# Forming one operand (T4) of a Strassen-type matmul by DMA: a copy and an accumulating transfer on the GpSimd queue, in place of one VectorE subtraction

## The chip, the cores and the metric

One core of one Trainium2 chip. The metric is the device time of one execution in microseconds (us). TensorE (PE) multiplies, VectorE (DVE) works elementwise, ScalarE (ACT) empties PSUM, GpSimd (POOL) does little but issue transfers here, and SyncE (SP) issues most transfers. Sixteen DMA engines serve all queues.

## The reference

```python
# x0: 16384 x 1024, ws: 6 x 1024 x 1024, bs: 6 x 1024, all bf16
x = x0
for l in range(6):
    proj = einsum('bd,de->be', x, ws[l]) + bs[l]
    x = x0 * proj + x
```

## The kernel before

The rows are cut into 16 pairs of blocks of 512 rows ("row pairs"). A *unit* is one layer of one row pair: 96 units. In a unit the product of x and the layer's weights is done by a Strassen-Winograd scheme with seven half-size products (P1 to P7) in place of eight; in 89 *steady* units P2 and P5 are split once more the same way. The units of the first row pair and the very last unit use one level only.

The scheme needs sums of blocks of x, formed on DVE, and sums of weight blocks. The weight sums are formed on DVE during the first row pair, stored to HBM (`Lc`), and loaded from there by all later pairs. Order on the engines is fixed by a table of ranks.

```python
B11, B12, B21, B22 = blk(xs, 0, 0), blk(xs, 0, 1), blk(xs, 1, 0), blk(xs, 1, 1)
ttop("T1", T[1][:], B12, B11, SUB, [XI[0, 1], XI[0, 0]], ["T1"])
ttop("T2", T[2][:], B22, T[1][:], SUB, [XI[1, 1], "T1"], ["T2"])
ttop("T3", T[3][:], B22, B12, SUB, [XI[1, 1], XI[0, 1]], ["T3"])
ttop("T4", T[4][:], B21, T[2][:], SUB, [XI[1, 0], "T2"], ["T4"])
# ... (cut)
for m in range(KH):
    group(f"P6.{m}", "6", pA[m], A[m], T[2], ["T2", A[m]], m, False)
    # ... P3, P7 and the emptying of PSUM (cut)
    group(f"P4.{m}", "4", pA[m], A[m], T[4], ["T4", A[m]], m, False)   # last group of a unit
```

Each tile T is 128 partitions x 2048 bf16 = 512 KB. x0 of the next row pair is loaded by transposing DMAs, and the finished x of the last row pair goes out by transposing DMAs and stores. All of these stand on SyncE's queue with the weight loads (nine of 512 KB per unit, into a ring of 16 tiles). They fall into the first three units of each row pair.

```python
if l == (2 if pr == 0 else 0) and nxt < NPAIR:
    for n in range(2):
        # ... x0 of the next pair, transposed on its way in
        op(base + 23 + n, ld, [], XN)
```

## Time and profile before

The time was 2276.61 us (2 runs, 2276.53 to 2276.68).

| one steady unit, 23.4 us | busy us |
|---|---|
| PE | 23.4 |
| DVE | 21.5 |
| ACT | 19.2 |
| POOL | 0 |

The page of the kernel before, in parts: busy time by engine; two DMA queues (packets, MB, share of the time of 16 engines; q1 is SyncE's, q0 GpSimd's); and the chain of work that ended last.

```profile
PE 2265.4 (100%) x12951; PEld 1264.0 (56%) x12951; DVE 2079.9 (91%) x2326; ACT 1839.4 (81%) x3228; POOL 22.1 (1%) x43
...
q1 hardware_dynamic: 618864, 534.58, 79.1%
q0 software_dynamic: 5184, 18.88, 2.2%
...
PE 98%; DVE 1%; SPq 0%; DMA 0%; issue 0%; ACT 0%; DVEq 0%
```

PE is busy all the time and is the chain. DVE is busy for 91% but is not on the chain. A DMA share is the sum of the packets' times; packets overlap, so it can pass 100%.

Groups by shape of the kernel before, DVE only (count, then busy us and mean ns). The first and the third line are T2 and T4 together, from x or, in layer 1, from x0.

```profile
L198 DVE TENSOR_TENSOR T<-xst,T 128x2048 bf16<-128x2048 bf16 x160 | 194.5, 1216 | 0.0
...
L198 DVE TENSOR_TENSOR T<-x0T 128x2048 bf16<-128x2048 bf16 x32 | 39.0, 1218 | 3.7 <-DMA x0T<-in_x_dram 3.7
L198 DVE TENSOR_TENSOR T<-x0T,T 128x2048 bf16<-128x2048 bf16 x32 | 38.9, 1216 | 0.1
```

The DMA engines' load is uneven. In the first units of a row pair the share is around or above 1; in layers 4 to 6 it is 0.62. The same view shows the second row pair, the first steady one:

```profile
160.00:180.00 20.00, 20.00 (x108) 10.33 (x107) 19.44 (x22) 16.72 (x30) 0.53 (x1) 1.00 1.08 369
180.00:200.00 20.00, 20.00 (x122) 11.78 (x121) 18.18 (x21) 17.46 (x31) 0.00 (x0) 1.00 1.17 255
200.00:220.00 20.00, 20.00 (x122) 11.65 (x121) 18.20 (x22) 16.66 (x30) 0.00 (x0) 1.00 1.12 271
220.00:240.00 20.00, 20.00 (x122) 11.74 (x121) 18.33 (x22) 17.16 (x31) 0.00 (x0) 1.00 1.05 389
240.00:260.00 20.00, 20.00 (x120) 11.55 (x119) 18.23 (x22) 15.97 (x29) 0.00 (x0) 1.00 0.75 255
```

Here the share is 1.05 or more for 80 us on end. The last weight sums have just been stored, and the ring of weight tiles fills from HBM at once.

### The profile page before, as it was taken

To read this page: it belongs to the slowest core of one execution; us is meant where nothing else is said; L and a number is where in the kernel's file an instruction comes from. 1 tells how busy PE (TensorE), PEld (TensorE's weight loads), DVE (VectorE), ACT (ScalarE), POOL (GpSimd) and SP (SyncE) were. 2 spreads that over 40 slices of the span, in tenths; PEclk is the share of its full clock that TensorE was granted. 3 is DMA by queue.
4 is the path that set the end of the run, shared out by engine and by line. 5 is a ranking of instruction groups with operands and counts; after the bars stand their busy time and mean duration, and the time that the engine had idled before them with its cause. 6 is when DMAs were issued, how large, how long until landed. Compare 5 with 4: busy or idle time off the path is not lost.

```text
span 2275.2 us, 34978 instructions
## 1 busy us (share of the span) xinstructions
PE 2265.4 (100%) x12951; PEld 1264.0 (56%) x12951; DVE 2079.9 (91%) x2326; ACT 1839.4 (81%) x3228; POOL 22.1 (1%) x43
## 2 busy tenths in 40 slices
PE   9999999999999999999999999999999999999998
PEld 4455555555555555555555555555555555555554
DVE  7999999999999999999999999999999999999997
ACT  5678888888888888888888888888888888888887
POOL 1110000000000000000000000000000000000000
PEclk9999999999999999999999999999999999999999
DMA  9779797796977969779697796978969689696872
GB/s 279 229 270 289 261 242 269 219 301 209 252 257 221 288 217 260 250 226 283 213 274 241 228 283 204 273 245 230 283 200 292 226 232 286 194 303 216 241 240 65
DMA packets 625868, 557.01 MB, mean 245 GB/s; under 512 B 397600, under 2 KB 552224, under 8 KB 625696
## 3 DMA queue, kind: packets, MB, share of 16 engines
q1 hardware_dynamic: 618864, 534.58, 79.1%
q0 software_dynamic: 5184, 18.88, 2.2%
q8 instruction: 101, 1.65, 0.3%
q10 hardware_dynamic: 1648, 1.32, 0.2%
q14 instruction: 71, 0.58, 0.1%
HBM read 436.22 MB, written 52.43 MB: 215 GB/s over the span
## 4 chain that ended last, share of the span: by engine, by line
PE 98%; DVE 1%; SPq 0%; DMA 0%; issue 0%; ACT 0%; DVEq 0%
PE pA L285 57%; PE pX L389 24%; PE pX L285 16%; DVE ev L198 1%; SPq L529 0%; DMA wp<-in_ws_dram 0%; DVE xst L198 0%; DVE T L198 0%; DVE ti L198 0%; DVE wp L198 0%; SPq L538 0%; ACT ev L294 0%; DVE x0T L487 0%; DVEq L608 0%; DVEq L198 0%
## 5 line engine op out<-in xcount | busy, mean ns | idle before, releaser
L285 PEld LDWEIGHTS <-wp 128*128 128x128 bf16 x7904 | 772.3, 98 | 843.7 <-issue 3.9
L285 PE MATMUL pA<-T,wp 128*128 128x512 bf16 x4608 | 1054.9, 379 | 0.5 <-DVE T L198 0.5
L294 ACT ACTIVATE ev<-pA,b_all 128x512 bf16<-128x512 f32 x1124 | 704.8, 690 | 211.8 <-PE pA L285 211.4
L389 PEld LDWEIGHTS <-wp 128*128 128x128 bf16 x4984 | 487.1, 98 | 156.6 <-issue 15.2
L198 DVE TENSOR_TENSOR ev<-ev,x0T 128x2048 bf16<-128x2048 bf16 (+2 forms) x484 | 482.7, 999 | 8.1 <-ACT ev L294 1.5
L198 DVE TENSOR_TENSOR xst<-ev,xst 128x2048 bf16<-128x2048 bf16 x319 | 388.9, 1219 | 18.6 <-DVE ev L198 0.5
L389 PE MATMUL pX<-ti,wp 128*128 128x256 bf16 x2848 | 397.6, 272 | 0.0
L198 DVE TENSOR_TENSOR ev<-ev,ev 128x2048 bf16<-128x2048 bf16 (+1 forms) x283 | 343.7, 1215 | 26.7 <-ACT ev L294 9.8
L294 ACT ACTIVATE ev<-pX,b_all 128x512 bf16<-128x512 f32 x412 | 289.4, 705 | 59.9 <-PE pX L285 49.3
L285 PE MATMUL pX<-xst,wp 128*128 128x512 bf16 x1376 | 336.4, 379 | 0.0
L285 PE MATMUL pA<-xst,wp 128*128 128x512 bf16 x1280 | 313.5, 379 | 0.0
L290 ACT COPY pX<-pA 128x512 f32<-128x512 f32 x412 | 256.3, 625 | 44.7 <-PE pA L285 44.3
L290 ACT CAST ev<-pX 128x512 bf16<-128x512 f32 x384 | 224.8, 619 | 49.0 <-ACT ev L294 37.6
L198 DVE TENSOR_TENSOR ev<-iu,ip 128x1024 bf16<-128x1024 bf16 x178 | 122.4, 688 | 120.7 <-ACT iu L290 120.7
L290 ACT COPY pX<-pX 128x512 f32<-128x512 f32 x356 | 208.7, 587 | 8.4
L290 ACT CAST iu<-pX 128x512 bf16<-128x512 f32 x356 | 196.8, 639 | 0.0
L198 DVE TENSOR_TENSOR T<-xst 128x2048 bf16<-128x2048 bf16 x160 | 194.8, 1217 | 0.3
L198 DVE TENSOR_TENSOR T<-xst,T 128x2048 bf16<-128x2048 bf16 x160 | 194.5, 1216 | 0.0
L389 PE MATMUL pX<-T,wp 128*128 128x256 bf16 x1068 | 160.2, 273 | 0.0
L290 ACT CAST ip<-pX 128x512 bf16<-128x512 f32 x178 | 104.7, 589 | 54.1 <-PE pX L389 54.1
L389 PE MATMUL pX<-xst,wp 128*128 128x256 bf16 x888 | 133.2, 273 | 0.0
L198 DVE TENSOR_TENSOR xst<-ev,x0T 128x2048 bf16<-128x2048 bf16 x64 | 78.2, 1222 | 1.6
(44 smaller groups left out, 624.3 us busy)
## 6 DMA issues: line engine op xcount, KB each, us to landing
wp<-Lc SPq DMA_DIRECT2D x538, 512.0 KB, 4.6
wp<-in_ws_dram SPq DMA_DIRECT2D x285, 512.0 KB, 5.3
out_dram<-x0T SPq DMA_DIRECT2D x30, 1024.0 KB, 8.6
Lc<-wp POOLq DMA_DIRECT2D x24, 512.0 KB, 6.2
Lc<-isum POOLq DMA_DIRECT2D x12, 512.0 KB, 6.9
w<-in_ws_dram SPq DMA_DIRECT2D x5, 512.0 KB, 6.3
wp<-in_ws_dram ACTq DMA_DIRECT2D x2, 512.0 KB, 5.8
out_dram<-x0T SPq DMA_DIRECT2D x2, 512.0 KB, 3.6
```

What stands on the lines that cost most here:

```text
L198: nc.vector.tensor_tensor(out=o, in0=a, in1=b, op=op)
L285: nc.tensor.matmul(bank[:], lhsT=wt[(u, w)][:, k, m * P:(m + 1) * P], rhs=rhs[:, k, :], start=(start and k == 0), stop=(k == KH - 1), skip ...
L290: add(name, lambda: nc.scalar.copy(out=dst, in_=src), rd, wr)
L294: add(name, lambda: nc.scalar.activation(out=dst, in_=src, func=IDENT, bias=b_all[:, c:c + 1], scale=1.0), rd, wr)
L389: nc.tensor.matmul(pX[bank][:, m * NQ:(m + 1) * NQ], lhsT=wv[:, k, m * P:(m + 1) * P], rhs=rhs[:, k, :], start=(start and m == 0 and k == ...
```

## The change

Intent: DVE is 91% busy, so take one of its operations out of each steady unit. T4 = x21 - T2 becomes x21 + (-T2). T2 is formed negated, and the weight sum that it is multiplied with is negated to match, which adds no operation. x21 is copied to T4 by a plain DMA as soon as it exists, and the negated T2 is added by an accumulating DMA.

```diff
-            combo("6", "5", "1", SUB, ("5",))
+            combo("6", "1", "5", SUB, ("5",))
...
-            combo("3", "2", "6", SUB, ("6",))
+            combo("3", "2", "6", ADD, ("6",))
...
-        ttop("T2", T[2][:], B22, T[1][:], SUB, [XI[1, 1], "T1"], ["T2"])
+        ttop("T2", T[2][:], T[1][:], B22, SUB, [XI[1, 1], "T1"], ["T2"])
...
-        ttop("T4", T[4][:], B21, T[2][:], SUB, [XI[1, 0], "T2"], ["T4"])
+        if one:      # one-level units
+            ttop("T4", T[4][:], B21, T[2][:], ADD, [XI[1, 0], "T2"], ["T4"])
+        else:
+            add("d4", lambda B21=B21: nc.gpsimd.dma_start(T[4][:], B21), [XI[1, 0]], ["T4"])
+            add("T4", lambda: nc.gpsimd.dma_start(out=T[4][:], in_=T[2][:], accum_op=ADD), ["T2", "T4"], ["T4"])
```

(The rank table gains an entry for the copy, `d4@3.3`. Lines below the change move down by four, so L389 is L393 after, L504 is L508.)

More of the change, by code (lines that the diff above doesn't have):

```diff
@@ L33 @@
 E4.2@23.01 E4.3@23.59
-T1@-1.14 5t13@0.59 5t2@3.06 2t13@3.39 5t4@5.13 2t2@6.6 T2@6.93 2t4@8.07 T4@8.4 5cc@10.88 T3@11.48 2cc@12.61 Q1@13.35
+d4@3.3 T1@-1.14 5t13@0.59 5t2@3.06 2t13@3.39 5t4@5.13 2t2@6.6 T2@6.93 2t4@8.07 T4@8.4 5cc@10.88 T3@11.48 2cc@12.61 Q1@13.35
 Qm@14.62 Qa@15.89 Ua@17.43 Um@18.7 Ux@19.97 Va@21.11 Wma@23.38 Wmb@24.58 Wx@25.31 Vm@27.38 Vx@28.85
@@ L115 @@
 E4.3@23.28 E4.2@23.85
-T1@-8.81 5t13@-7.54 2t13@-6.94 2t2@-5.20 T2@-4.87 5t2@-3.40 5t4@.36 T4@2.97 2t4@5.58 T3@6.85 2cc@12.32 Q1@13.06
+d4@3.3 T1@-8.81 5t13@-7.54 2t13@-6.94 2t2@-5.20 T2@-4.87 5t2@-3.40 5t4@.36 T4@2.97 2t4@5.58 T3@6.85 2cc@12.32 Q1@13.06
 Qm@14.33 5cc@15.47 Qa@16.07 Ua@17.41 Um@18.68 Ux@19.95 Va@21.08 Wma@23.45 Wmb@24.66 Wx@25.40 Vm@27.47 Vx@28.94
@@ L126 @@
 E4.1@22.74 E4.2@23.61
-T1@-1.18 5t13@.65 5t2@3.13 2t13@3.47 5t4@5.20 2t2@6.67 T2@7.01 2t4@8.14 T3@8.48 T4@9.61 2cc@12.46 Q1@13.20 Qm@14.47
+d4@3.3 T1@-1.18 5t13@.65 5t2@3.13 2t13@3.47 5t4@5.20 2t2@6.67 T2@7.01 2t4@8.14 T3@8.48 T4@9.61 2cc@12.46 Q1@13.20 Qm@14.47
 5cc@15.61 Qa@16.21 Ua@17.45 Um@18.72 Ux@19.99 Va@21.12 Wma@23.49 Wmb@24.69 Wx@25.43 Vm@27.50 Vx@28.97
```

## The prediction

> **What bounds the kernel.** TensorE. The page has PE busy 2265.4 of 2275.2 us (100%) at a granted clock of 0.999; the chain of waits is 98% PE, 1% DVE. A steady unit takes 23.44 us (the timeline repeats at that distance); a window of 23.40 us has 23.40 us of PE, 21.55 of DVE, 19.25 of ACT, none of POOL. DVE's one idle spell in a unit is 1.37 us, waiting for ACT.
>
> **What the change removes.** 89 DVE operations (one per steady unit), 1.216 us each by the groups by shape: 108 us, so DVE falls from 91% to about 87%. First-pair units and the last unit keep their DVE T4. The built programs show PE order unchanged, and DVE order unchanged but for the 89 missing rows. None of this is on the chain, so removing it saves nothing. The swapped operands cost nothing.
>
> **What it adds.** 178 transfers of 512 KB on the GpSimd queue. POOL spends 0.53 us on each (36 such stores in the trace, issued while DVE was busy): 94 us on an idle engine. On the DMA engines one plain 512 KB store took 2.2% x 2275 / 36 = 1.4 us of all 16. The accumulating one must read two operands (the Trainium skill, "Collectives: The Full Stack", The bandwidth ceiling: the add needs two source reads); I estimate 2.8 us from the plain one. No accumulating transfer is in the trace before, so this is the weakest number. Together 89 x 4.2 = 374 us, DMA share from 82% to about 98%. That share is no ceiling: windows reach 1.25, and rates reach 399 GB/s against a mean of 245, so the weight traffic still fits. Weights are loaded some 30 us before use (issue times of SyncE against the units), and SyncE waits over 1,300 us for buffers to come free, so a delay of a few us is absorbed.
>
> **The deadline of T4.** From a unit's start: x21 is ready by +3.2, so the copy is issued at about +3.3 and lands, at the 6.2 us of the queue's stores, at about +9.5. T2 ends at +8.2. The accumulating transfer then runs from +9.5 to about +16.5. The first P4 matmul starts at +20.0: slack 3.5 us; before it was 10.3. In light stretches (DMA share 0.6) it should be larger; in three of six units (transposes, output stores; share 1.0 to 1.25, median landings of 8 to 9 us) it may vanish, and PE then waits 1 to 3 us in some units. I expect 0 to 30 us in all.
>
> **Prediction: 2279 us, 8 times in 10 within 2271 to 2315. Faster by over 2%: 0.01; within 2%: 0.85; slower by over 2%: 0.14.**
>
> **What would show it.** PE still about 100% busy, DVE down by 108 us, its idle time up by as much, in a gap after T2; POOL about 94 us more; the GpSimd queue's share up by some 16 points. Deadline step: the landing times of the two new transfers, and little or no idle time of PE that ends with a DMA into T. Weight step: no PE idle released by weight loads.
>
> **What would make it wrong.** (a) The accumulating transfer is much slower than two reads suggest (say 10 us of all engines): then every P4 waits, or the DMA engines run out, and the time rises by 5% or more. (b) Descriptor generation on GpSimd is held up by DVE's two-input operations; the 0.53 us speaks against it. (c) The heavy stretches delay T4 in half the units. A gain above 0.5% would mean DVE did hold PE up somewhere, which the waits do not show.

## More of the kernel before

Windows of one unit each, for four units of one row pair: layers 2, 3, 4, 5. Columns are length; PE, weight loads, DVE, ACT and POOL busy (with the number of instructions); granted clock, the share of its full clock that PE was given; DMA share; GB/s.

```profile
459.90:483.30 23.40, 23.40 (x138) 13.27 (x137) 21.51 (x25) 19.24 (x35) 0.00 (x0) 1.00 1.14 273
483.30:506.70 23.40, 23.40 (x137) 13.30 (x136) 21.51 (x26) 19.24 (x35) 0.00 (x0) 1.00 1.00 359
506.70:530.20 23.50, 23.50 (x138) 13.34 (x137) 21.61 (x26) 19.35 (x35) 0.00 (x0) 1.00 0.62 202
530.20:553.60 23.40, 23.40 (x137) 13.29 (x136) 21.52 (x26) 19.25 (x35) 0.00 (x0) 1.00 0.63 203
```

## The result, and the profile after

The changed kernel took 2302.98 us (2 runs, 2299.06 and 2306.9), a ratio of 1.0115 [1.0086, 1.0145]. A ratio is the mean time of one kernel's fast runs over that of the other's in the same rounds, so it is not quite the ratio of the quoted medians. Five more rounds (below) gave 2301.15 us against 2277.15. So the change costs 24 to 26 us, 1.0 to 1.2%.

The page after, in the same parts:

```profile
PE 2271.5 (99%) x12951; PEld 1263.7 (55%) x12951; DVE 1980.4 (86%) x2237; ACT 1839.7 (80%) x3228; POOL 149.1 (6%) x221
...
q1 hardware_dynamic: 618864, 534.58, 76.4%
q0 software_dynamic: 30816, 112.21, 17.9%
```

DVE is down by 99.5 us (89 operations of 1.216 us are 108 us, but consecutive ones overlap: they start 1.14 us apart), POOL is up, and q0 has 17.9% where it had 2.2%. That is (0.179 x 2305 - 0.022 x 2275) / 89 = 4.07 us of all 16 engines per T4; the prediction estimated 4.2.

DVE's idle time in a unit, by the timeline, before and then after (start, length, engine, line, operation; in brackets the idle time ahead of it and what ended it):

```profile
846.00 0.69 DVE L198 TENSOR_TENSOR ev<-iu,ip 128x1024 bf16<-128x1024 bf16 x1 [1.37 <-ACT iu L290]
```

```profile
866.11 0.69 DVE L198 TENSOR_TENSOR ev<-iu,ip 128x1024 bf16<-128x1024 bf16 x1 [2.52 <-ACT iu L290]
```

The time that was freed is 1.15 us more of waiting for ACT, at the place where T4 was formed. PE is the loser. The waits of PE and of its weight loads (PEld) in the change's trace: who, for whom, total us, times, longest us.

```profile
PEld L285 <- DMA wp<-Lc: 15.5, 2, 13.7
...
PE pA L285 <- DMA wp<-Lc: 13.2, 1, 13.2
...
PE pA L285 <- DMA T<-T: 8.0, 8, 2.1
...
PE pA L285 <- ACT ev L294: 1.0, 2, 0.8
```

None of these waits for DMA stands in the trace before. The two lines for `wp<-Lc` tell of one event at 221 to 234 us, seen by the weight load and by the matmul behind it (the weight load's line also counts a wait of 1.8 us at 175 us). In PE's timeline of the change:

```profile
219.05 1.90 PE L285 MATMUL pX<-xst,wp 128*128 128x512 bf16 x8
234.16 8.96 PE L285 MATMUL pA<-T,wp 128*128 128x512 bf16 x32 [13.21 <-DMA wp<-Lc]
```

PE stood still for 13.2 us, for one tile of weights. The 32 matmuls after it took 8.96 us where 32 of the same take 7.07 (line 197.26 of this timeline), because the clock had been halved. The Trainium skill ("TensorE: Matmul & The Clock Gate", The HAM clock gate) says that an idle PE falls to half clock and needs about 3.4 us of work to come back. The trace agrees: the two windows of 10 us from 220 to 240 us show a granted clock of 0.72 and 0.60.

SyncE's queue tells why that tile was late. Its timeline before, then after:

```profile
200.48 11.04 SPq L504 DMA_TRANSPOSE x0T<-in_x_dram  x2
211.62 0.53 SPq L246 DMA_DIRECT2D wp<-Lc  x1
```

```profile
207.57 15.96 SPq L508 DMA_TRANSPOSE x0T<-in_x_dram  x2
223.63 0.53 SPq L246 DMA_DIRECT2D wp<-Lc  x1
```

The load that PE waited for (issued at 223.63 and landed at 234) stands behind two transposing loads of x0. They were begun 7 us later and took 5 us longer to issue than before. So the load was issued 12 us later than it had been, and it landed (completed) after 10.5 us where it had taken 3.8. There was little room for that. In the trace before, this tile landed at 215.4 and its matmuls began at 218.46: a lead of 3.0 us, where the same tile of the third unit of the fourth row pair had 15.7.

The other waits are T4s that came late. The issue view of the change gives the median time from issue to landing:

```profile
T<-T POOLq DMA_DIRECT2D x89, 512.0 KB, 8.8
T<-xst POOLq DMA_DIRECT2D x74, 512.0 KB, 5.5
```

I laid the two traces side by side, unit by unit, by the start of each P1. Of the 29.8 us between these two profiled executions 15.3 us arise in the third unit of the second row pair, 1.5 us in its first unit, 0.8 us at the start of the kernel, and about 12 us in a dozen units scattered over the rest, 0.2 to 4 us each. Counted from a unit's start ("+" in what follows), the accumulating transfer landed at a median of +17.8 us (layers 4 to 6) and +18.2 us (layers 1 to 3); P4 begins at +20.0. Fifteen of 89 landed after +19.9. The nine of these in layers 4 to 6 were all in layer 4.

One of them shows the price of a short wait:

```profile
1531.59 3.62 PE L285 MATMUL pA<-T,wp 128*128 128x512 bf16 x16
1537.31 5.30 PE L285 MATMUL pA<-T,wp 128*128 128x512 bf16 x16 [2.10 <-DMA T<-T]
```

The wait was 2.10 us, but the 16 matmuls after it took 5.30 us where 16 take 3.62: the clock was halved for 3.4 us. The unit lost 3.95 us in all.

### The profile page after: what moved, and what is told of

Read it like the earlier page. It is cut to its first block, busy times and chain, and to the rows that moved or that the text cites. A ratio compares the mean times of both kernels' runs of the same rounds, so it can differ in the third digit from the quotient of the medians.

```text
span 2305.0 us, 35322 instructions
## 1 busy us (share of the span) xinstructions
PE 2271.5 (99%) x12951; PEld 1263.7 (55%) x12951; DVE 1980.4 (86%) x2237; ACT 1839.7 (80%) x3228; POOL 149.1 (6%) x221
## 3 DMA queue, kind: packets, MB, share of 16 engines
q0 software_dynamic: 30816, 112.21, 17.9%
## 5 line engine op out<-in xcount | busy, mean ns | idle before, releaser
L285 PE MATMUL pA<-T,wp 128*128 128x512 bf16 x4608 | 1060.6, 380 | 22.9 <-DMA wp<-Lc 13.2
L393 PEld LDWEIGHTS <-wp 128*128 128x128 bf16 x4984 | 487.0, 98 | 156.6 <-issue 15.0
L198 DVE TENSOR_TENSOR ev<-ev,x0T 128x2048 bf16<-128x2048 bf16 (+2 forms) x484 | 483.2, 1000 | 17.9 <-ACT ev L294 11.3
L198 DVE TENSOR_TENSOR xst<-ev,xst 128x2048 bf16<-128x2048 bf16 x319 | 389.1, 1220 | 18.1 <-DVE ev L198 0.5
L393 PE MATMUL pX<-ti,wp 128*128 128x256 bf16 x2848 | 397.6, 272 | 0.0
L393 PE MATMUL pX<-T,wp 128*128 128x256 bf16 x1068 | 160.2, 273 | 0.0
L393 PE MATMUL pX<-xst,wp 128*128 128x256 bf16 x888 | 133.2, 273 | 0.0
L351 POOL DMA_DIRECT2D T<-xst x74 | 41.1, 555 | 1238.4 <-DVE ti L198 1224.4
L352 POOL DMA_DIRECT2D T<-T x89 | 77.6, 872 | 528.8 <-DVE T L198 228.5
```

The source lines that it names most:

```text
L198: nc.vector.tensor_tensor(out=o, in0=a, in1=b, op=op)
L285: nc.tensor.matmul(bank[:], lhsT=wt[(u, w)][:, k, m * P:(m + 1) * P], rhs=rhs[:, k, :], start=(start and k == 0), stop=(k == KH - 1), skip ...
L351: add("d4", lambda B21=B21: nc.gpsimd.dma_start(T[4][:], B21), [XI[1, 0]], ["T4"])
L352: add("T4", lambda: nc.gpsimd.dma_start(out=T[4][:], in_=T[2][:], accum_op=ADD), ["T2", "T4"], ["T4"])
L393: nc.tensor.matmul(pX[bank][:, m * NQ:(m + 1) * NQ], lhsT=wv[:, k, m * P:(m + 1) * P], rhs=rhs[:, k, :], start=(start and m == 0 and k == ...
```

## The experiments

"Before" is the kernel before, run in the same rounds: 2277.15, 2278.07 and 2277.45 us for runs 1 to 4, 5 to 8 and 9 to 12. All runs had five rounds. The record marks every run's result as right, also those of runs 5 and 12, which compute a wrong T4; so for these two the mark says nothing.

I began with theory A: weights starve once, in the first steady row pair, because loads stand behind slow transposes; the rest is late T4s. Its rivals: B, late T4s alone; C, an even slowdown by the DMA load.

### 1. The change again

No edit.

> The change as it stands, for more executions. In its first profile PE lost about 30 us: 15.3 us in one unit of the second row pair (a wait of 13.2 us for a weight load, then a halved clock), about 1.5 us there for a late T4, some 12 us in a dozen other units for late T4s. Theory A (weights starve once, in the first steady pair): 2295 to 2308 us in every execution, with one wait of PE for a weight load of over 8 us near 221 us. Rival B (late T4 alone; the long wait was an accident of one execution): most executions at 2288 to 2292, no such wait.

Measured: 2301.15 us (2299.43 to 2302.15), 24.0 us slower than before. The trace again has a wait for a weight load near 221 us:

```profile
PE pA L285 <- DMA wp<-Lc: 8.4, 1, 8.4
PE pA L285 <- DMA T<-T: 7.3, 4, 2.3
```

The third unit of the second row pair lost 11.4 us. So the long wait recurs, with a size that varies, and every execution is at 2299 us or more.

### 2. and 3. The second row pair alone, undone and done

```diff
-        if one:
+        if one or pr == 1:      # run 2
+        if one or pr != 1:      # run 3
```

> T4 of the six units of the second row pair back on DVE, the other 83 units by DMA. Theory A: about 16 us faster than the change, 2284 to 2291 us, and no long wait of PE for weights. Rival B (late T4s everywhere): only 2 us faster. Rival C (the DMA load slows everything evenly): 6 of 89 units, 2 us.

Measured: 2289.48 us (2283.8 to 2291.48), 11.7 us faster than the change, and no wait of PE for a weight load from `Lc`.

> The reverse: T4 by DMA in the six units of the second row pair alone. Theory A: about 15 us slower than the kernel before (2290 to 2294 us), with the one long wait for weights. Rivals B and C: at most 2 us slower.

Measured: 2290.14 us (2287.39 to 2291.06), 13.0 us slower than before, with the wait:

```profile
PE pA L285 <- DMA wp<-Lc: 5.2, 1, 5.2
...
PE pA L285 <- DMA T<-T: 1.2, 1, 1.2
```

Six of 89 units make half of the loss. Both numbers are a little under A's expectation, which came from the execution with the longest wait. B and C are refuted as the whole cause. The two halves add up: 13.0 (run 3) and 12.3 (run 2 over before) against 24.0 for the whole.

### 4. and 11. The transposes of that pair moved

```diff
-        if l == (2 if pr == 0 else 0) and nxt < NPAIR:
+        if l == (2 if pr < 2 else 0) and nxt < NPAIR:
```

Run 4 is the change with this; run 11 is run 3 with this.

> The change, with the two transposing loads of the third row pair's x0 put behind 17 weight loads on SyncE's queue, that is about two units later, in the second row pair only. Same transfers, same bytes. Theory A with its cause as I read it (weight loads wait on SyncE's queue behind transposes that take longer to issue): the long wait for weights goes, 2284 to 2292 us. Rival A2 (the DMA engines are simply out of capacity in this stretch, whatever the order): the wait stays, within 4 us of the change.

Measured: 2297.59 us (2292.59 to 2301.1), 3.6 us faster than the change. That is A2's side of the line, and A's expectation missed. The long wait for weights did go: the longest is 2.8 us, and the tile that PE had waited for landed at +8.4, not +25 to +30. But the first unit of the pair now lost 4.2 us to a T4 2.35 us late and the clock after it.

> T4 by DMA in the second row pair alone, with the x0 transposes there moved behind 17 weight loads. Without the move this was 13 us slower than before, with a wait of 5.2 us for a weight load and a halved clock after it. If the queue order of SyncE makes that wait, it goes and 2 to 6 us of late T4s stay (2279 to 2284 us); if it is the DMA engines' capacity alone, PE waits elsewhere and the loss stays within 3 us (2287 to 2291 us).

Measured: 2289.53 us (2285.55 to 2292.5), 12.1 us slower than before, within 1 us of run 3. The wait for the weight load shrank from 5.2 to 1.8 us, and another came up one unit later. PE's and POOL's timelines of run 11:

```profile
252.00 6.12 PE L285 MATMUL pA<-T,wp 128*128 128x512 bf16 x16 [5.66 <-DMA x0T<-in_x_dram]
```

```profile
237.96 0.88 POOL L352 DMA_DIRECT2D T<-T  x1 [7.52 <-DVE ev L198]
```

The profile puts PE's wait down to an x0 load. But these matmuls are P4, which reads T4 and not x0; and the accumulating transfer issued at 237.96 took 13.9 us, so it landed at 251.9, when PE went on. The moved x0 loads, at a median of 18.1 us to landing in this window, now share the engines with it.

So the second half of A's cause holds for that wait, but not for the loss. The order on SyncE's queue decides which transfer is late, and little of how much is lost: run 11 lost as much as run 3, and run 4 only 3.6 us less than the change (in its profile the second pair lost 6.6 us, against 13.8 in run 1). That the DMA engines' capacity is what is short fits this, in a stretch whose DMA share was above 1 for 80 us before anything was added. It is argued and not shown: run 5, where the bytes stay and the engines' time goes down, lost 7.9 us in the third unit, and run 3, with the accumulations, lost 7.7 there.

### 5. The accumulation replaced by a plain copy (wrong result)

```diff
-nc.gpsimd.dma_start(out=T[4][:], in_=T[2][:], accum_op=ADD)
+nc.gpsimd.dma_start(out=T[4][:], in_=T[2][:])
```

> Wrong result on purpose: the second transfer is a plain copy of T2 over T4, not an accumulating one; same number, order and waits. It should take 1.3 us of all 16 engines where the accumulating one took 2.6. Theory: it lands 2 to 4 us sooner, near +14 to +16 in a unit, so the late T4s (about 12 us) go nearly all: 2286 to 2296 us, more if the wait for weights shrinks too. Rival (latency of the queue, not the accumulation, makes T4 late): landing times within 1 us of the change's, late T4s stay.

Measured: 2293.69 us (2292.27 to 2298.56), 7.5 us faster than the change. GpSimd's queue and the waits of PE:

```profile
q0 software_dynamic: 30816, 112.21, 12.7%
```

```profile
PE pA L285 <- DMA wp<-Lc: 5.2, 1, 5.2
...
PE pA L285 <- DMA T<-T: 2.3, 3, 1.3
```

Packets and bytes are those of the change; the queue's share is 12.7 against 17.9%. So accumulating costs (0.179 x 2305 - 0.127 x 2292) / 89 = 1.4 us more of 16 engines than copying. With 4.07 us for both transfers, that is 1.35 us for a copy and 2.7 for an accumulation. The Trainium skill ("Collectives: The Full Stack", The bandwidth ceiling) says of the add in a reduce-scatter that it needs two source reads; a factor of two is what this shows for an accumulating transfer. The transfer landed 2 us sooner (+15.8 and +16.3), the waits for T4 fell from 7.3 (run 1) to 2.3 us, and the loss in the third unit of the second pair was 7.9 us.

The time is in the expected range, but the late T4s did not go. Eleven of 89 still landed after +19.9 (nine in run 1), ten of them in layer 3, where the copy ahead of the second transfer took a median of 8.5 us to land (5.1 in run 1). So the slow accumulation is not the only reason for a late T4: a late copy is another.

### 6. and 7. Quiet units and busy units

```diff
-        if one:
+        if one or pr == 1 or l < 3:     # run 6: DMA in layers 4 to 6 alone
+        if one or pr == 1 or l >= 3:    # run 7: DMA in layers 1 to 3 alone
```

> T4 by DMA only in the units of layers 4 to 6 (no transposes, no output stores) of row pairs 3 to 16, 41 units; DVE elsewhere. The prediction held that T4 comes late in the busy units and not here: then within 2 us of the kernel before. The change's trace has 9 late T4s in such units, median landing at +17.8 against the need at +19.9: then 3 to 8 us slower than before.

Measured: 2276.99 us (2276.87 to 2277.66); ratio 0.9996 [0.9983, 1.0008]. Not one T4 was late. The prediction's view held here, and what I expected from the trace did not.

```profile
T<-xst POOLq DMA_DIRECT2D x41, 512.0 KB, 2.9
T<-T POOLq DMA_DIRECT2D x41, 512.0 KB, 9.1
```

> The complement: T4 by DMA only in the units of layers 1 to 3 (transposes, output stores) of row pairs 3 to 16, 42 units. By the prediction nearly all of the late T4s: 10 to 30 us slower than before. By the change's trace (6 late T4s in such units, one of them in the second pair): 2 to 6 us slower.

Measured: 2282.8 us (2278.85 to 2283.12), 4.7 us slower than before; ratio 1.0015. Four T4s landed after +19.9, all in layer 3. One of them was 2 us late, and most of the profiled loss (3.8 of 5.8 us) was that one and the clock after it:

```profile
1210.36 5.30 PE L285 MATMUL pA<-T,wp 128*128 128x512 bf16 x16 [1.99 <-DMA T<-T]
```

Both together (run 2) cost 12.3 us; apart they cost -1.1 and 4.7. The costs do not add up, so the two kinds of unit act on each other. That gave theory D: the transfers of busy units push the weight loads behind, and the T4 of the next unit meets loads that are catching up.

### 8. and 12. The control, and the saving without the cost

Run 8 keeps the negated T2 and forms T4 by an addition on DVE everywhere (`if True:` for `if one:`). Run 12 leaves T4 out of the steady units altogether (wrong result):

```diff
-        else:
-            add("d4", ...)
-            add("T4", ...)
```

> Control: the swapped operands stay (negated T2, weight sums to match), T4 is an addition on DVE everywhere, no new transfer. All theories: the kernel before within 1 us. If it differs, the operand swap does something and every other run has to be read against this one.

Measured: 2277.55 us (2277.09 to 2279.74); ratio 0.9999. The operand swap does nothing.

> Wrong result on purpose: T4 is not formed at all in the 89 steady units (P4 reads an old T4), no DVE operation and no transfer. This is the change's saving without its cost. The prediction: DVE is off the chain, so 2276 to 2278 us, no gain at all. If DVE did hold PE up somewhere, it is faster than the kernel before by more than 2 us.

Measured: 2277.3 us (2277.03 to 2277.5); ratio 0.9999 [0.9986, 1.0011].

```profile
PE 2253.7 (99%) x12713; PEld 1264.2 (56%) x12951; DVE 1978.6 (87%) x2237; ACT 1841.6 (81%) x3228; POOL 22.1 (1%) x43
...
q0 software_dynamic: 5184, 18.88, 2.2%
```

(This trace has 12,713 of 12,951 matmul records, so its PE sum is low.) DVE lost its 89 operations, the DMA queues are those of before, and no time was saved. So no way of taking T4 off DVE, however cheap, can make this kernel faster.

### 9. and 10. The units after the busy stretch

```diff
-        if one:
+        if one or pr == 1 or l == 3:         # run 9: layer 4 on DVE too
+        if one or pr == 1 or l in (2, 3):    # run 10: layers 3 and 4 on DVE too
```

> T4 by DMA in all units but those of the second row pair and those of layer 4, the first unit after the busy stretch (69 of 89 units by DMA). New theory D: late T4s come from backlog. The transfers of the busy units push the weight loads behind, and the T4 of layers 3 and 4 then shares the DMA engines with loads catching up. So taking the 14 layer-4 transfers out, of 83, takes out the 8 late T4s that the trace of the run with the second pair on DVE shows there: 4 to 8 us faster than that run's plus 12 us, so 2280 to 2285 us. Rival E (every T4 by DMA has the same small chance of being late): 17% of 12 us, so 2286 to 2289 us.

Measured: 2283.08 us (2282.68 to 2287.37), 5.6 us slower than before. Taking 14 of 83 transfers out of run 2 took out 6.4 us of about 12. D's range held, E's did not. In the trace no T4 of layers 5 and 6 landed late, and four each of layers 2 and 3 did.

> As the run before, with layer 3 on DVE too: 55 of 89 units by DMA, those of layers 1, 2, 5 and 6. Theory D: no T4 is late any more, within 1.5 us of the kernel before, although 62% of the change's transfers stand. Rival E: 55/83 of 12 us, some 8 us slower than before.

Measured: 2278.57 us (2277.27 to 2279.55), 1.1 us slower than before; ratio 1.0004 [0.9992, 1.0017]. The view of waits has none of PE for T4 left, though 55 of 89 T4s are formed by DMA; a single one landed late, at +20.2, and its unit lost 0.4 us. D held again in time.

The traces show both steps of D, though no run tests them one by one. In runs 2 and 7 the nine weight loads of layer 4 landed 8 to 11 us later, counted from the unit's start (medians of row pairs 3 to 16), than in the kernel before and in run 6. And in run 2 the copy of layer 4 took a median of 7.2 us to land where it took 2.9 in run 6, so the accumulating transfer was issued at +11.4 and not at +8.5. It then took no longer than in run 6 (8.6 against 9.0 us). So in layer 4 it is the plain copy that comes late. That the weight loads are what slows it is not shown by itself.

No version beats the kernel before, and run 12 says why none of this kind can.

## Why the prediction was right or wrong

The forecast (within 2%; 2271 to 2315 us) held, but its middle of 2279 us was 24 us low, and one of its steps failed. That the range held is partly luck: it was made wide for late T4s (0 to 30 us), and about half of the loss came from late weights, which the prediction had ruled out.

- **"None of this is on the chain, so removing it saves nothing"; "the swapped operands cost nothing."** Right. Shown by runs 12 and 8.
- **The cost of the transfers, 1.4 + 2.8 us of 16 engines.** Right: 1.35 + 2.7. The DMA share rose from 82% to 95% of the span, not quite to 98%.
- **"Weights are loaded some 30 us before use ... so a delay of a few us is absorbed."** This step failed. I had read it from a row pair in mid-run and taken it for all. In the second row pair the ring has no such lead: one tile of its third unit had 3.0 us in the trace before, and the change brought it to PE 13 us too late. The DMA share is above 1 for 80 us already, and PE waited 5 to 13 us for weights (runs 1 and 3, the change), plus half a clock after that. The pair is worth about 13 us (run 3), some 1.4 of it a late T4 in its first unit. "Weight step: no PE idle released by weight loads" was the test, and the trace fails it.
- **The deadline: landing at +16.5, slack 3.5 us.** Mis-sized: the accumulating transfer takes 8.8 us from issue to landing, not 7, and lands at +18. The slack is 2 us. In layer 4 it is gone: there the copy is issued at +3.7 and takes 7.2 us, not 6.2, so the accumulation is issued at +11.5 and lands at +20.0. "0 to 30 us in all" for late T4s held: 12 us (run 2).
- **"In light stretches it should be larger; in three of six units it may vanish."** Half right. Quiet units alone have no late T4 (run 6). But with the busy units' transfers there as well, layer 4, the first quiet unit, is late most often (runs 2, 9, 10).
- **What I left out:** the clock. A wait of about 2 us was in some cases followed by 3.4 us at half clock, which nearly doubles its price.
- **(b) descriptor generation held up by DVE.** No sign of it. POOL was busy for 0.555 us per copy, always with DVE busy, and for 0.872 us per accumulation, the same in the 14 with DVE busy throughout as in those with DVE mostly idle. POOL rose by 127 us, not by 94, because an accumulation was taken to cost what a plain transfer does (0.53 us).

## What to carry to other kernels

An engine at 91% that is not on the chain had nothing to give here: leave the operation out altogether, wrong result and all, and time it before looking for another place for it. Moving work to the DMA engines spends a resource with its own schedule, so read its share stretch by stretch, the first steady stretch above all, and not as a mean: the mean was 82% here, and half of the loss came from a stretch that was over 100% for 80 us on end before the change. Count every transfer of a chain, too: here a plain copy that came late made the accumulation behind it late. In this kernel a PE wait of 2 us cost up to 4 us, for the clock.

## What the Trainium skill lacked or had wrong

- "DMA: Bandwidth & Descriptors" says that an accumulating DMA goes through GpSimd, but gives no time for one. Here 512 KB of bf16 from SBUF onto SBUF took 2.7 us of 16 engines against 1.35 for a plain copy (pages of the change and of run 5), 0.87 against 0.555 us of POOL, and 8.8 against 5.5 us from issue to landing.
- "TensorE: Matmul & The Clock Gate" (HAM oscillation) says to have no PE-idle gaps over about 3.4 us. Here gaps of 1.99 us (run 7) and 2.10 us (the change) were each followed by 16 matmuls that took 1.7 us longer, while one of 2.04 us (run 2, at 1521 us) was not. In all, in the nine traces that have gaps over 0.7 us ahead of such matmuls (those that read a T, after 160 us), none of 29 gaps of 0.7 to 1.8 us had slow matmuls after it, five of seven gaps of 1.99 to 2.35 us did, and so did all five of 5.2 us or more. The page says in Part 1 that its window runs freely, so the phase may decide; no run here tests that.
